# DeltaNet and PReLU feed-forward: the eighth chunk's first product in seven-product form

## The chip, the cores and the metric

The kernel runs on one core of a Trainium2 chip. Its engines are TensorE (PE; PEld is its weight load), VectorE (DVE), ScalarE (ACT), GpSimd (POOL) and SyncE (SP, which issues transfers). The metric is the device time of one execution in microseconds (us), as the median of several runs; lower is better.

## The reference, cut to what matters

```python
batch, n_heads, seq, head_dim = (4, 8, 768, 48)
k_n = k / (np.linalg.norm(k, axis=-1, keepdims=True) + 1e-06)
for t in range(S):
    kt, vt, bt = (k_n[:, :, t], v[:, :, t], beta[:, :, t, None])
    y[:, :, t] = np.einsum('bhd,bhde->bhe', q[:, :, t], state)
    v_old = np.einsum('bhde,bhd->bhe', state, kt)
    state = state + bt[:, :, :, None] * np.einsum('bhd,bhe->bhde', kt, vt - v_old)
# x: y as 3072 tokens of 384; w_in 384 x 2048, w_out 2048 x 384, all float32
h = x @ w_in
g = np.maximum(h, 0.0) + alpha * np.minimum(h, 0.0)
return (g @ w_out).astype(np.float32)
```

A recurrent attention whose state is corrected at each token, then a feed-forward block with a slope `alpha` of its own for each hidden feature below zero.

## The kernel before, in words

The sequence is cut into 12 chunks of 64 positions; with four batches a chunk has 256 tokens. Attention goes through 24 steps `n`, two per chunk (one per pair of batches). Inside a step the recurrence is a triangular system. Four steps share one elimination on DVE (`eliminate`, L594 a product and L600 a sum, 30 times each, then transposes to `turned` and `inverse`, L567), done ahead in small pieces. Each step has a burst A (through the state, outputs, next state: PE L868, L906, L925) and a burst B (L792, L850, and L893, whose result DVE turns into `u` at L897). L792 multiplies with `diag`, which ACT copies from `turned` (L765).

The feed-forward part of chunk c has a first product (`x @ w_in`, 16 blocks of 128 features, taken in eight pairs) and a second (`g @ w_out`). It fills PE between the bursts. `feed_forward` is a generator over all chunks; `stretch` and `weave` lay its pieces, the elimination's pieces and small copies between the bursts at shares written out by hand (`FILL`, `FILLS`: pieces of feed-forward; `PIECES_OF`, `TURNS`: pieces of elimination for the three stretches of a step). All five engines run in the order in which the code issues, so an instruction that waits holds up what is queued behind it on its engine.

The plain first product (`ffn_in`, L1071) has six matmuls of 256 columns per pair; ACT then writes relu(-h) from PSUM (L1081) and DVE forms alpha' times that plus h in two halves (L1083), where alpha' is 1 - alpha. The seven-product form (`ffn_in_fast`) treats two of the three blocks of 128 along the inner dimension as a two by two block product with seven products in place of eight: per pair two matmuls of 256 columns (L1311), three of 128 (L1316) and four shared ones of 128 (L1321) into another PSUM bank `q`. ACT copies these four to SBUF as `z` (L1340), POOL adds them up in three instructions (L1345), DVE adds them to the pair's own PSUM bank to get h (L1350, `total`), ACT writes relu(-h) to `r` (L1355, `below`) and DVE applies the slopes (L1359, `slope`). The list `Due` lays these at steps after the pair. The form needs sums of blocks of `w_in` (`input_sums`, L1238, eight DVE instructions, which write into attention buffers no longer used and into `w_in`) and four sums of tokens (`token_sums`, L1273). One bank `q` serves all pairs but the first, so a pair's shared products wait for ACT's copy of the pair before.

`FAST_IN = 8`: chunks 0 to 7 (the first eight) use the plain form, chunks 8 to 11 the seven-product form. The second products of chunks 2 and later are in a seven-product form of their own (`ffn_out_fast`, L1135, DVE additions L1159, sums of activations L1025; `ffn_out_faster`, L1405 and L1401, behind `ffn_in_fast`). The input sums are made in the second product of chunk 7, every third step.

In `ffn_in_fast` the buffers for `z` alternate between a spare key tile and half of the elimination's `block`, those for `r` between another key tile and `block`'s other half. `rows_y` copies a step's outputs to `xt` in 16 small ACT instructions (L962), behind DVE's transpose `z` (L949).

Of the kernel before, what the change touches and what calls it, by code (L numbers as in the profile page):

```python
# [25 lines left out]
FP32 = mybir.dt.float32  # L26
U32 = mybir.dt.uint32
S8 = mybir.dt.int8
ALU = mybir.AluOpType
# [4 lines left out]
HB = 32  # L34
W_IN_P = 512
BUSY = 8
EARLY = 8
FIRST = 6
NARROW = 8
LATE = 16  # L40
FAST_IN = 8


@with_exitstack
def kernel(
# [11 lines left out]
    nc = tc.nc  # L57

    B, H, S, D = q.shape
# [6 lines left out]
    G = H // 2  # L66
# [4 lines left out]
    const = ctx.enter_context(tc.tile_pool(name="const", bufs=1))  # L71
    work = ctx.enter_context(tc.tile_pool(name="work", bufs=2))
    psum = ctx.enter_context(tc.tile_pool(name="psum", bufs=1, space=bass.MemoryType.PSUM))

    doubles, big, ffn_banks = ExitStack(), [], []
# [54 lines left out]
    k_early = [k_pair[:, 0], k_pair[:, 1], k_last]  # L130
# [169 lines left out]
    for t in range(2):  # L300
# [5 lines left out]
        out=ones, in_=ones, compare_op=ALU.is_ge, fill=1.0, base=0,  # L306
# [7 lines left out]
    for t in range(2):  # L314
# [5 lines left out]
        out=first_of, in_=ident.rearrange("p (q u e) -> p u q e", u=2, e=HB // 2)[:, 0],  # L320
# [39 lines left out]
    inv = [const.tile([128, H, C], FP32, name=f"inv{i}") for i in range(NE)]  # L360
    mid = [const.tile([128, H, C], FP32, name=f"mid{i}") for i in range(2)]

    right = [const.tile([128, H + 1, HB], FP32, name=f"right{i}") for i in range(EARLY)]

    def zeros():

# [162 lines left out]
    NJ = 4  # L529
# [456 lines left out]
    FP = FT // 2  # L986
# [215 lines left out]

    held = {}

    def spare():

        if not held:
            held["same"] = work.tile([128, NJ, H, HB], FP32, name="same", bufs=1)
            for i in range(3):
                held[i] = work.tile([128, G, 128], FP32, name="k_t", bufs=EARLY + 1)  # L1210
        return held

    def input_sum(x, h):

        def four(t):
            return t.rearrange("p h d -> p (h d)").rearrange("p (i e) -> p i e", e=128)

        if x == 0:
            flat = spare()["same"].rearrange("p j h c -> p (j h c)")
            return flat.rearrange("p (i e) -> p i e", e=128)[:, 4 * h : 4 * h + 4]  # L1220
        if x == 1:
            return four(k_early[h])
        return four(k_early[2]) if h == 0 else spare()[0]

    def input_sums():

        for h in range(2):
            own = [
                w_in[:, t].rearrange("p (i f e) -> p i f e", f=2, e=128)[:, 4 * h : 4 * h + 4]
                for t in range(2)  # L1230
            ]
            a11, a12, a21, a22 = own[0][:, :, 0], own[1][:, :, 0], own[0][:, :, 1], own[1][:, :, 1]
            s1, s2, s3 = (input_sum(x, h) for x in range(3))
            for dst, x, y, op in (
                (s1, a21, a22, ALU.add), (s2, s1, a11, ALU.subtract),
                (s3, a11, a21, ALU.subtract), (a21, a12, s2, ALU.subtract),
            ):
                nc.vector.tensor_tensor(out=dst, in0=x, in1=y, op=op)  # L1238
                yield

    class Due:

# [18 lines left out]

    def token_sums(c):

        xt, t = xts[c], spare()[2]

        def x(k, u):
            return xt[:, k, u * 128 : (u + 1) * 128]

        for dst, a, b in (
            (0, x(0, 1), x(0, 0)), (1, x(1, 1), t[:, 0]), (2, x(1, 1), x(0, 1)),  # L1270
            (3, x(1, 0), t[:, 1]),
        ):
            nc.vector.tensor_tensor(out=t[:, dst], in0=a, in1=b, op=ALU.subtract)  # L1273

    def ffn_in_fast(c):
        xt = xts[c]
        gss[c] = [act_of(c, i) for i in range(FP)]
        due = due_of[c] = Due()
        t = spare()[2]

        def x(k, u):
            return xt[:, k, u * 128 : (u + 1) * 128]

        def quarter(flat):
            return flat.rearrange("p (i e) -> p i e", e=128)

        def terms(i):

            if i % 2 == 0:
                return spare()[1]  # L1290
            if "block" not in held:
                held["block"] = work.tile([128, HB * (HB + 1)], FP32, name="block", bufs=1)
            return quarter(held["block"][:, 0:512])

        def pair(i):
            p = ffn_banks[i % 3]
            q = quarter(ffn_banks[2 if i == 0 else 3])
            z, g = terms(i), act_of(c, i)
            if "less" not in held:
                held["less"] = work.tile([128, G, 128], FP32, name="k_t", bufs=EARLY + 1)  # L1300
            r = held["less"] if i % 2 == 0 else quarter(held["block"][:, 512:1024])
            r = r.rearrange("p (f u) e -> p f (u e)", f=2)

            def w(k, f):
                return w_in[:, k, (2 * i + f) * 128 : (2 * i + f + 1) * 128]

            def s(x):
                return input_sum(x, i // 4)[:, i % 4]

            def whole(f):  # L1310
                nc.tensor.matmul(  # L1311
                    p[:, f * 256 : f * 256 + 256], w(2, f), xt[:, 2], start=True, stop=False
                )

            def more(j, a, b):
                nc.tensor.matmul(  # L1316
                    p[:, j * 128 : j * 128 + 128], a, b, start=False, stop=(j > 0)
                )

            def shared(j, a, b):  # L1320
                nc.tensor.matmul(q[:, j], a, b, start=True, stop=True)  # L1321

            def own():
                whole(0)
                yield
                more(0, w(1, 0), x(1, 0))
                more(1, w(0, 1), x(1, 1))
                yield
                whole(1)
                yield  # L1330
                more(2, w(1, 1), t[:, 3])
                yield

            def common():
                shared(0, w(0, 0), x(0, 0))
                shared(1, s(1), t[:, 1])
                yield
                shared(2, s(2), t[:, 2])
                shared(3, s(0), t[:, 0])
                nc.scalar.copy(z, q)  # L1340
                for dst, a, b in (
                    (z[:, 1], z[:, 0], z[:, 1]), (z[:, 2], z[:, 1], z[:, 2]),
                    (z[:, 1::2], z[:, 1:3], z[:, 3:4].to_broadcast([128, 2, 128])),
                ):
                    nc.gpsimd.tensor_tensor(out=dst, in0=a, in1=b, op=ALU.add)  # L1345
                yield

            def total():
                h = g.rearrange("p f i -> p (f i)")
                nc.vector.tensor_tensor(  # L1350
                    out=h, in0=p, in1=z.rearrange("p i e -> p (i e)"), op=ALU.add
                )

            def below():
                nc.scalar.activation(r, g, ACT.Relu, scale=-1.0)  # L1355

            def slope():
                for f in range(2):
                    nc.vector.scalar_tensor_tensor(  # L1359
                        out=g[:, f], in0=r[:, f], scalar=al_t[:, 2 * i + f : 2 * i + f + 1],  # L1360
                        in1=g[:, f], op0=ALU.mult, op1=ALU.add,
                    )

            due.put(PER * (i + 1) + {0: PER, FP - 1: 2}.get(i, 3), total)
            due.put(PER * (i + 2) + {FP - 2: 1, FP - 1: -4}.get(i, 2), below)
            due.put(PER * (i + 2) + {FP - 2: 1, FP - 1: -2}.get(i, 5), slope)
            for gen in (own(), common()) if i == 0 else (common(), own()):
                for _ in gen:
                    due.step()
                    yield  # L1370

        early = operand_sums(0)
        due.put(PER * 6 + 5, lambda: next(early, None))
        rest = chain(early, operand_sums(1))
        for at in (6, 6, 7, 7, 8, 9, 10):
            due.put(PER * FP + at, lambda: next(rest, None))
        for i in range(FP):
            yield from pair(i)
# [604 lines left out]
    )  # L1983

    def feed_forward():
        for c in range(2, FAST_IN):
            yield from ffn_in(c)
            if c < FAST_IN - 1:
                yield from ffn_out_fast(c)
        made = input_sums()  # L1990
        for i, _ in enumerate(ffn_out_fast(FAST_IN - 1)):
            if i > 2 and i % 3 == 0:
                next(made, None)
            if i == FAST_PARTS - 2:
                assert FAST_IN in whole
                token_sums(FAST_IN)
            yield
        for _ in made:
            assert False
        for c in range(FAST_IN, NCH):  # L2000
            yield from ffn_in_fast(c)
            yield from ffn_out_faster(c)
# [10 lines left out]
    for n in range(NJ, JOINED):  # L2013
# [9 lines left out]
        JOINED: (3, WHOLE - 2 * PIECES - 6 - 2 * share - 3, 2 * PIECES),  # L2023
        JOINED + 1: (0, 4, 7), JOINED + 2: (4, 5, 7), JOINED + 3: (1, 1, 6),
    }
    TURNS = [(3, 3, 4), (3, 3, 4), (4, 4, 4), (0, 5, 6)]
    FILL = {JOINED: (8, 12, 12), JOINED + 1: (10, 12, 10), JOINED + 2: (8, 10, 12)}
    FILLS = [(12, 10, 12), (12, 18, 12)]
# [94 lines left out]
```

## Time and profile before

| | |
|---|---|
| median of 3 runs | 631.03 us (630.53 to 634.83) |
| the profiled execution | 630.72 us, of which the span is 629.0 |
| eighth chunk (c = 7), first product | 407.03 to 433.61 us |
| its second product | 433.61 to 453.8 us |
| ninth chunk (c = 8), first product, seven-product form | 453.8 to 479.04 us |
| bursts of steps 16 B, 17 A, 17 B | 407.89, 415.03, 429.93 us |
| bursts of steps 18 A, 18 B, 19 A | 438.81, 454.64, 461.46 us |
| POOL additions L1345 | 96, 56.4 us in all, 28.4 and 28.0 by buffer |

The profile shows, per engine, the busy time; a chain of waits from the end backwards; and a timeline of instructions, with the idle time in front of them and what ended it. A matmul of float32 leaves two records.

### The profile page before, as it was taken

The page shows a single profiled execution, that of the slowest core. Times are in us where ns is not written, and L with a number is a line of the kernel's source. Part 1 is how long each engine was busy: PE and PEld are TensorE (multiplying, and loading weights), DVE is VectorE, ACT ScalarE, POOL GpSimd, SP SyncE. Part 2 cuts the span into 40 slices and gives each one's busy share as a digit, 9 for nine tenths or more (in the row PEclk, how much of TensorE's full clock was granted, in tenths as well). Part 3 has the DMA queues.
Part 4 walks back from the last instruction along what each step waited for, and adds up shares of the span by engine and source line. Part 5 has one row for each costly group of instructions (what it writes and reads, how often), then busy time and mean ns, then how long its engine had stood idle before and what let it go on. Part 6 is the DMA issues. An engine that isn't in the chain of part 4 may idle for free.

```text
span 629.0 us, 21661 instructions
## 1 busy us (share of the span) xinstructions
PE 617.6 (98%) x9116; PEld 546.5 (87%) x9116; DVE 502.5 (80%) x1219; ACT 312.2 (50%) x834; POOL 98.5 (16%) x214
## 2 busy tenths in 40 slices
PE   6999999999999999999999999999999999999997
PEld 5678888566789989989989989989999999999997
DVE  4988898979989988868978868778979578486383
ACT  6878566255545146347346446335356366352230
POOL 7031211010001000000000000000053062071350
PEclk9999999999999999999999999999999999999999
DMA  7968735112243341241332221311220300100100
GB/s 117 302 151 175 253 76 162 29 40 52 41 78 52 63 67 28 55 73 28 54 69 34 43 37 26 56 26 24 49 49 12 62 15 12 29 3 1 26 1 25
DMA packets 145968, 39.26 MB, mean 62 GB/s; under 512 B 139040, under 2 KB 142256, under 8 KB 145872
## 3 DMA queue, kind: packets, MB, share of 16 engines
q1 hardware_dynamic: 144000, 37.40, 29.1%
q8 instruction: 71, 1.16, 0.7%
q10 hardware_dynamic: 1872, 0.49, 0.4%
q14 instruction: 25, 0.20, 0.1%
HBM read 33.14 MB, written 4.72 MB: 60 GB/s over the span
## 4 chain that ended last, share of the span: by engine, by line
PE 89%; DVE 5%; ACT 2%; DMA 1%; SPq 1%; issue 1%; ACTq 0%; DVEq 0%
PE p_ffn L1071 18%; PE p_ffn L1135 10%; PE p_more L1071 8%; PE p_more L1405 8%; PE p_more L1135 8%; PE p_more L1321 5%; PE p_ffn L1114 5%; PE p_ffn L1311 3%; PE p_ffn L1405 3%; PE p_pair L868 3%; PE p_ffn L1316 3%; PE p_pair L906 2%; PE p_pair L792 2%; PE p_pair L502 2%; PE p_pair L850 2%; PE p_pair L728 2%
## 5 line engine op out<-in xcount | busy, mean ns | idle before, releaser
L1071 PE MATMUL p_ffn<-xt,w_in 128*128 128x256 f32 x528 | 123.1, 384 | 0.1
L1071 PEld LDWEIGHTS p_ffn<-xt,w_in 128*128 128x128 f32 x528 | 97.7, 190 | 14.0 <-ACT inv L762 0.4
L962 ACT COPY xt<-z 32x96 f32<-32x96 f32 x240 | 64.5, 269 | 49.6 <-DVE z L949 46.4
L1071 PE MATMUL p_more<-xt,w_in 128*128 128x256 f32 x240 | 55.7, 382 | 0.0
L1345 POOL TENSOR_TENSOR k_t<-k_t 128x128 f32<-128x128 f32 (+1 forms) x48 | 28.4, 592 | 165.8 <-ACT k_t L1340 163.3
L600 DVE TENSOR_TENSOR block<-block,prod 128x30 f32<-128x30 f32 (+9 forms) x150 | 50.0, 333 | 5.1
L1071 PEld LDWEIGHTS p_more<-xt,w_in 128*128 128x128 f32 x240 | 44.9, 190 | 6.3
L594 DVE TENSOR_TENSOR prod<-block 128x30 f32<-128x30 f32 (+9 forms) x150 | 48.6, 324 | 1.3
L419 POOL TENSOR_TENSOR beta_t<-beta_t,rec 128x8 f32<-128x8 f32 x24 | 7.0, 294 | 244.2 <-DVE rec L413 240.1
L1083 DVE SCALAR_TENSOR_TENSOR act<-act,al_t,p_ffn 128x256 f32<-128x256 f32 x72 | 31.0, 471 | 16.3 <-ACT act L1081 16.3
L809 ACT COPY inv<-p_pair 32x256 f32<-32x256 f32 x30 | 10.9, 362 | 59.1 <-DVE u L897 35.5
L1081 ACT ACTIVATE act<-p_ffn 128x512 f32<-128x512 f32 x36 | 21.4, 594 | 25.4 <-PE p_ffn L1071 25.1
L1345 POOL TENSOR_TENSOR block<-block 128x128 f32<-128x128 f32 (+1 forms) x48 | 28.0, 583 | 12.8 <-ACT block L1340 10.3
L1311 PE MATMUL p_ffn<-xt,w_in 128*128 128x256 f32 x96 | 29.3, 387 | 0.0
L1135 PE MATMUL p_ffn<-w_out,act 128*128 128x192 f32 x160 | 27.7, 327 | 0.0
L1135 PEld LDWEIGHTS p_ffn<-w_out,act 128*128 128x128 f32 x160 | 26.2, 190 | 0.3
L897 DVE TENSOR_TENSOR u<-p_pair,wgt 128x384 f32<-128x384 f32 x24 | 13.2, 553 | 16.5 <-PE p_pair L893 9.2
L1083 DVE SCALAR_TENSOR_TENSOR act<-act,al_t,p_more 128x256 f32<-128x256 f32 x40 | 17.3, 474 | 10.9 <-ACT act L1081 10.8
L878 DVE TENSOR_TENSOR r<-v_raw,p_pair 64x192 f32<-64x192 f32 (+1 forms) x66 | 23.2, 352 | 2.1 <-PE p_pair L868 1.0
L1135 PE MATMUL p_more<-w_out,act 128*128 128x192 f32 x128 | 22.3, 326 | 0.0
L1340 ACT COPY k_t<-p_more 128x512 f32<-128x512 f32 x16 | 9.4, 586 | 25.5 <-PE p_more L1321 18.9
L1405 PE MATMUL p_more<-w_out,act 128*128 128x192 f32 x128 | 21.5, 327 | 0.0
(279 smaller groups left out, 1480.8 us busy)
## 6 DMA issues: line engine op xcount, KB each, us to landing
w_out<-in_moe_w_in_dram SPq DMA_DIRECT2D x10, 512.0 KB, 5.6
v_raw<-in_v_dram SPq DMA_DIRECT2D x48, 96.0 KB, 2.8
kl<-in_k_dram SPq DMA_DIRECT2D x96, 48.0 KB, 2.4
out_dram<-o_sb SPq DMA_DIRECT2D x90, 48.0 KB, 1.6
space_out<-in_moe_w_out_dram SPq DMA_DIRECT2D x11, 384.0 KB, 4.5
ke_last<-in_k_dram SPq DMA_DIRECT2D x25, 96.0 KB, 3.3
qp<-in_q_dram SPq DMA_DIRECT2D x64, 32.0 KB, 2.2
w_out<-in_moe_w_out_dram SPq DMA_DIRECT2D x5, 384.0 KB, 6.2
```

The costliest lines, as they stand in the source:

```text
L594: nc.vector.tensor_tensor(out=prod, in0=r[:, 0:j, j : j + 1].to_broadcast([128, j, n]), in1=r[:, j : j + 1, j + 1 : HB].to_broadcast([128, ...
L600: nc.vector.tensor_tensor(out=r[:, 0:j, j + 1 : HB], in0=r[:, 0:j, j + 1 : HB], in1=prod, op=ALU.add)
L878: nc.vector.tensor_tensor(out=r[to, a], in0=v_in[to, a], in1=p[own, a, :, 0:D], op=ALU.subtract)
L962: nc.scalar.copy(to[quad(r), u, bp, t], z[quad(2 * t + u), r])
L1071: nc.tensor.matmul(p_h[:, i], w_in[:, t, (f + i) * 128 : (f + i + 1) * 128], xt[:, t], start=(t == 0), stop=(t == KT - 1),)
L1083: nc.vector.scalar_tensor_tensor(out=g[:, i], in0=g[:, i], scalar=al_t[:, f + i : f + i + 1], in1=p_h[:, i], op0=ALU.mult, op1=ALU.add,)
L1114: nc.tensor.matmul(p_o[u], gs[f // 2][:, f % 2, u * 128 : (u + 1) * 128], w_out[:, f], start=(f == 0), stop=(f == FT - 1),)
L1135: nc.tensor.matmul(p, x(i), w(i), start=(i == 0), stop=(i == FP - 1))
L1311: nc.tensor.matmul(p[:, f * 256 : f * 256 + 256], w(2, f), xt[:, 2], start=True, stop=False)
L1321: nc.tensor.matmul(q[:, j], a, b, start=True, stop=True)
L1345: nc.gpsimd.tensor_tensor(out=dst, in0=a, in1=b, op=ALU.add)
L1405: nc.tensor.matmul(p, x(i), w(i), start=(i == 0), stop=(i == FP - 1))
```

## The change

1. `FAST_IN` goes from 8 to 7: the eighth chunk's first product takes the seven-product form, so the input sums must be made a chunk earlier, in the second product of chunk 6. The two sums that overwrite `w_in` come last, and the eight are laid at steps 1, 3, 5, 8, 11, 14, 18 and 22 in place of every third. The spare tiles are taken one by one when first needed.
2. `z` and `r` of pair i share one buffer, the activation tile of pair i + 2; the last two pairs use the space of two `right` tiles and a key tile. `right` becomes one tile cut into eight.
3. In chunk 7 alone, for the first six pairs, ACT multiplies `r` by the slopes (two instructions), and DVE's `slope` is one addition over both halves.
4. `ffn_banks` is rotated by one before the first chunk of the new form.
5. The elimination's pieces are laid differently in steps 15, 16 and 18: (0, 5, 1), (1, 3, 4), (8, 7, 4) in place of (0, 5, 6), (3, 3, 4), (4, 4, 4).

```diff
-FAST_IN = 8
+FAST_IN = 7
...
-    right = [const.tile([128, H + 1, HB], FP32, name=f"right{i}") for i in range(EARLY)]
+    rights = const.tile([128, EARLY, H + 1, HB], FP32, name="right")
+    right = [rights[:, i] for i in range(EARLY)]
...
     def input_sums():
 
+        last = []
         for h in range(2):
...
                 (s1, a21, a22, ALU.add), (s2, s1, a11, ALU.subtract),
-                (s3, a11, a21, ALU.subtract), (a21, a12, s2, ALU.subtract),
+                (s3, a11, a21, ALU.subtract),
             ):
                 nc.vector.tensor_tensor(out=dst, in0=x, in1=y, op=op)
                 yield
+            last.append((a21, a12, s2))
+        for dst, x, y in last:
+            nc.vector.tensor_tensor(out=dst, in0=x, in1=y, op=ALU.subtract)
+            yield
...
         def terms(i):
 
-            if i % 2 == 0:
-                return spare()[1]
-            if "block" not in held:
-                held["block"] = work.tile([128, HB * (HB + 1)], FP32, name="block", bufs=1)
-            return quarter(held["block"][:, 0:512])
+            if i < FP - 2:
+                return quarter(act[:, i + 2].rearrange("p f i -> p (f i)"))
+            if i == FP - 1:
+                return spare(1)
+            return quarter(rights[:, 0:2].rearrange("p n h i -> p (n h i)")[:, 0:512])
...
-            if "less" not in held:
-                held["less"] = work.tile([128, G, 128], FP32, name="k_t", bufs=EARLY + 1)
-            r = held["less"] if i % 2 == 0 else quarter(held["block"][:, 512:1024])
-            r = r.rearrange("p (f u) e -> p f (u e)", f=2)
+            r = z.rearrange("p (f u) e -> p f (u e)", f=2)
+            scaled = c < FAST_IN + 1 and i < FP - 2
...
             def below():
                 nc.scalar.activation(r, g, ACT.Relu, scale=-1.0)
+                if scaled:
+                    for f in range(2):
+                        nc.scalar.mul(r[:, f], r[:, f], al_t[:, 2 * i + f : 2 * i + f + 1])
 
             def slope():
+                if scaled:
+                    nc.vector.tensor_tensor(out=g, in0=r, in1=g, op=ALU.add)
+                    return
                 for f in range(2):
...
     def feed_forward():
+        made, m = input_sums(), FAST_IN - 1
+        at = {(m, 1): (1, 3, 5, 8, 11, 14, 18, 22)}
         for c in range(2, FAST_IN):
...
+            for k, passes in enumerate((ffn_in(c), ffn_out_fast(c))):
+                for i, _ in enumerate(passes):
+                    if i in at.get((c, k), ()):
+                        next(made)
+                    if (c, k, i) == (m, 1, FAST_PARTS - 2):
+                        assert FAST_IN in whole
+                        token_sums(FAST_IN)
+                    yield
         for _ in made:
             assert False
+        ffn_banks.append(ffn_banks.pop(0))
         for c in range(FAST_IN, NCH):
             yield from ffn_in_fast(c)
             yield from ffn_out_faster(c)
...
+    PIECES_OF.update({15: (0, 5, 1), 16: (1, 3, 4), 18: (8, 7, 4)})
```

More of the change, by code (lines that the diff above doesn't have):

```diff
@@ L1203, with spare @@
     held = {}
[L1205 to L1211, printed above, removed]
+    def spare(i):
+        if i not in held:
+            held[i] = (
+                work.tile([128, NJ, H, HB], FP32, name="same", bufs=1) if i == "same"
+                else work.tile([128, G, 128], FP32, name="k_t", bufs=EARLY + 1)
+            )
+        return held[i]
     def input_sum(x, h):
@@ L1218, in input_sum @@
         if x == 0:
-            flat = spare()["same"].rearrange("p j h c -> p (j h c)")
+            flat = spare("same").rearrange("p j h c -> p (j h c)")
             return flat.rearrange("p (i e) -> p i e", e=128)[:, 4 * h : 4 * h + 4]
@@ L1222, in input_sum @@
             return four(k_early[h])
-        return four(k_early[2]) if h == 0 else spare()[0]
+        return four(k_early[2]) if h == 0 else spare(0)
     def input_sums():
+        last = []
         for h in range(2):
@@ L1262, in token_sums @@
     def token_sums(c):
-        xt, t = xts[c], spare()[2]
+        xt, t = xts[c], spare(2)
         def x(k, u):
@@ L1278, in ffn_in_fast @@
         due = due_of[c] = Due()
-        t = spare()[2]
+        t = spare(2)
         def x(k, u):
@@ L1985, in feed_forward @@
     def feed_forward():
+        made, m = input_sums(), FAST_IN - 1
+        at = {(m, 1): (1, 3, 5, 8, 11, 14, 18, 22)}
         for c in range(2, FAST_IN):
[L1987 to L1997, printed above, removed]
+            for k, passes in enumerate((ffn_in(c), ffn_out_fast(c))):
[6 more added lines that the diff above has]
+                    yield
         for _ in made:
             assert False
+        ffn_banks.append(ffn_banks.pop(0))
         for c in range(FAST_IN, NCH):
```

## The prediction

> **What bounds the kernel now.** The page's first part comes first, then the chain that ended last, in order of time. Columns of the chain: start, length, what (one matmul leaves two records).
>
> ```profile
> PE 617.6 (98%) x9116; PEld 546.5 (87%) x9116; DVE 502.5 (80%) x1219; ACT 312.2 (50%) x834; POOL 98.5 (16%) x214
> ...
> 421.30 5.18 PE p_ffn L1071 x24
> ...
> 454.64 0.68 PE p_pair L792 x50
> ...
> 465.84 0.43 PE p_ffn L1311 x2
> ...
> 468.27 0.43 PE p_ffn L1311 x2
> ```
>
> From 100 us on PE hardly idles. A plain first product costs 5.18/24 = 0.216 us a record. One seven-product pair runs from 465.84 to 468.27, 2.43 us. So PE's work is the bound, and only as long as DVE, ACT and POOL deliver in time. Busy time by stage tells how close they are. The first two rows are the eighth chunk's first product, the third is its second product, the fourth the ninth chunk's first product, already in the new form. Columns: PE, PEld, DVE, ACT, POOL.
>
> ```profile
> 407.00:427.00 20.00, 20.00 (x301) 17.26 (x300) 15.35 (x38) 6.87 (x18) 0.00 (x0) 1.00 0.19 39
> 427.00:434.00 7.00, 7.00 (x154) 6.08 (x153) 6.02 (x16) 3.48 (x10) 0.00 (x0) 1.00 0.20 25
> 434.00:454.00 20.00, 20.00 (x208) 19.60 (x207) 19.26 (x45) 9.34 (x33) 0.00 (x0) 1.00 0.19 31
> 454.00:479.00 25.00, 25.00 (x496) 23.50 (x496) 19.75 (x39) 15.29 (x37) 13.70 (x24) 1.00 0.23 42
> ```
>
> DVE is full in the third row, and POOL is idle in the first three. The timeline of DVE, ACT and POOL gives the deadlines and what POOL does to DVE. Columns: start, length, engine, line, operation, and in brackets the idle time before it and what ended it.
>
> ```profile
> 449.75 0.59 DVE L567 STREAM_TRANSPOSE turned<-block 128x256 f32<-128x256 f32 x1
> ...
> 467.47 1.35 DVE L1359 SCALAR_TENSOR_TENSOR act<-block,al_t,act 128x256 f32<-128x256 f32 x2
> ...
> 472.01 1.58 DVE L1359 SCALAR_TENSOR_TENSOR act<-block,al_t,act 128x256 f32<-128x256 f32 x2
> ...
> 478.45 0.87 DVE L1359 SCALAR_TENSOR_TENSOR act<-block,al_t,act 128x256 f32<-128x256 f32 x2
> ```
>
> ```profile
> 450.37 0.41 ACT L765 COPY diag<-turned 128x256 f32<-128x256 f32 x1 [1.34 <-DVE turned L567]
> ```
>
> ```profile
> 466.54 2.00 POOL L1345 TENSOR_TENSOR block<-block 128x128 f32<-128x128 f32 x3 [2.37 <-ACT block L1340]
> ...
> 471.46 1.85 POOL L1345 TENSOR_TENSOR block<-block 128x128 f32<-128x128 f32 x3 [0.65 <-ACT block L1340]
> ```
>
> The last elimination's result reaches `diag` at 450.78, and step 18's burst on PE (L792) wants it at 454.64: 3.86 us to spare. A pair of slopes (L1359, both tensors in SBUF) takes 0.87 us with POOL at rest and 1.35 and 1.58 beside POOL's additions at 466.54 and 471.46.
>
> **The change part by part.**
>
> PE. The eighth chunk's first product has 96 records, 96 x 0.2157 = 20.70 us without the attention bursts. In the new form it is what the twelfth chunk shows, which has no burst in it: from 587.89, where the second product before it ends, to 607.30, 19.41 us. Gain 1.3 us, all of it on the path. The number of weave steps is 48 in both forms, so the bursts fall at the same places.
>
> ACT. Added: eight copies of shared products (L1340, 0.586) and twelve scalings by alpha; for these the nearest row is L762, 128x256 with a per-partition scale, 0.51. That is 4.7 + 6.1 = 10.8 us where ACT is busy 10.35 of 27 us: covered as a sum. The order is less comfortable. ACT's queue has three copies of `xt` ahead of the sixth pair's copy of shared products, they wait for DVE's transpose `z`, and pair 7's shared products on PE wait for that one bank. In the ninth chunk the same copy ends at 471.39 and PE wants the bank at 472.23: 0.84 us to spare.
>
> POOL. 24 additions, 8 x 1.8 = 14.4 us, in a stage where POOL was idle. Their own cost is hidden by that; what they cost DVE is priced below.
>
> Input sums. Eight of 0.60 us (start to start, L1238) move to the seventh chunk's second product. By the instruction order, five elimination steps fewer lie in that stretch. From the solve of step 15 to that of step 16 DVE's work goes from 18.5 to 18.9 us (rows times spacings) in 24.7 us: hidden by its idle time, 0.4 us if that cover were gone. The buffers they write have no later reader in the attention part; the queue of transfers keeps its order. Nothing.
>
> Buffers. Shared products go to later activation tiles, `right` becomes one tile with the same addresses, the banks are rotated by one so that the numbering fits one chunk less. A pair's buffer is no longer reused two pairs later, which takes waits away and adds none on PE; the addition that overwrites a tile comes after the slope that reads it on the same engine. Nothing; at worst one POOL addition late, 0.46 us.
>
> DVE, from the solve of step 16 (409.65) to the fourth transpose `turned`. Added: seven elimination steps (deferred from the stretches before) at 0.75 = 5.2; eight totals at 0.60, six one-piece slopes at 0.60 and two old pairs at 0.79 in place of eight pairs at 0.79, +3.7; three output additions that now precede it, 0.27 each, +0.8. Removed: five input sums, -3.0. Net +6.7 us. To swallow it there are the 3.86 us above, less the 1.3 by which PE comes sooner, and DVE's idle 1.96 + 0.67 + 1.15 + 0.15 = 3.9 us; but the first total must wait for the first shared products and POOL's additions. In the ninth chunk it starts 4.3 us after the solve, DVE has 3.2 us of work until then, so 1.0 us stays idle. 6.7 - 2.5 - 2.9 = 1.3 us short. The wait is PE's, at step 18's burst, and behind it stands the ninth chunk.
>
> DVE beside POOL. In that stretch 25 DVE instructions with two SBUF operands (18 of the elimination, 6 slopes, one sum) fall where POOL adds. The ninth chunk's eight pairs of slopes take 0.87, 1.35, 1.08, 1.58, 1.54, 0.87, 0.88, 0.88: 2.1 us over 8 x 0.87, or 0.13 an instruction; 25 x 0.13 = 3.3. Elimination steps beside POOL's copies early in the kernel are nearer in kind but not in what POOL does: L600 took 0.440 in place of 0.349 and 0.450 in place of 0.378 us, 0.08 more; with the 40 in 64 slopes that met POOL, 25 x 0.63 x 0.08 = 1.3. Upper end: the 40 slopes beside POOL average 0.710 us against 0.478 for the other 24, 25 x 0.232 = 5.8. Lower end 0: DVE may wait anyway. I take the middle of the two nearer rows, 2.3 us, since most of the 25 are elimination instructions and the POOL work is that of the slopes' row.
>
> The Trainium skill, page "SBUF — State Buffer", section "SBUF: two separate sides", says that VectorE instructions with two SBUF inputs and GpSimd instructions exclude each other on one pair of ports, for a whole instruction. The trace agrees: the totals (L1350), with one operand in PSUM, keep 0.68 us beside POOL. By that rule every one of the 25 would pay like the slopes that met POOL, and the sum would end near the upper end.
>
> Sum, against the profiled execution (630.72 us, span 629.0 and 1.7 around it; 0.3 below the median 631.03): -1.3 + 1.3 + 2.3 = +2.3, **633.0 us**.
>
> **The rivals.**
>
> Cover holds (not slower). DVE's idle time and spare take all of it, say because the lock costs nothing beyond waits that exist and the deferred steps fit. For it: before, DVE ran 2.2 us behind PE (output additions at 450.78 for products that ended at 448.57) and PE did not wait. Against it: the 1.3 us are short before any contention. 630.72 - 1.3 = 629.4 us, up to 630.4.
>
> POOL and DVE exclude each other fully. 25 x 0.232: 630.72 - 1.3 + 1.3 + 5.8 = 636.5 us. For it: the slopes' rows. Against: elimination instructions are shorter, and some of their waiting falls into waits between a product and the sum that needs it.
>
> ACT's order binds. DVE's `z` comes 1.2 us later than in the ninth chunk, relative to PE, which is 0.4 over the 0.84 to spare, and 14 of the 25 instructions precede it (1.3 us): PE waits 1.7 us at pair 7's shared products, and afterwards DVE catches up. 630.72 - 1.3 + 1.7 = 631.1 us.
>
> The change not doing what it says is no rival with weight: PE's instruction order has the 24 further matmuls, and the form's time is measured in four chunks.
>
> **How the numbers follow.** Forecast 0.45, its own range 631.5 to 635.5 (lock 0.8 to 4.8); cover holds 0.30; ACT's order 0.10; full exclusion 0.15. The range 629.2 to 636.0 leaves out about half of the full exclusion and 0.1 of tails. One per cent, 6.3 us, is about what a measurement of this kernel can tell from no change: faster than 624.7 would need a gain that PE's records do not hold, 0.01; slower than 637.3 only beyond the full exclusion, 0.05; within, 0.94.
>
> **What would show it.** Right: L1071 down by 96 records and the seven-product lines up by 144; PE's chain broken at L792 in step 18 by `diag` and DVE's `turned`, perhaps earlier at pair 7's shared products; elimination rows (prod, block) between 412 and 433 us longer than now; DVE without idle time from there to 455. Wrong: no idle PE between 407 and 460, or waits of PE anywhere before 400, which nothing here foresees. What would overturn the sum is the DVE count: a few instructions that overlap more than their spacings say.

## The result, and the profile after

The changed kernel takes 635.28 us (median of 8 runs, 633.87 to 637.31) against 631.12 us before (8 runs, 630.09 to 634.83): ratio 1.0061, interval 1.0037 to 1.0085. The profiled execution took 633.87 us, of which the span is 632.2. So it got slower by about 4 us; 633.0 was forecast.

The shares of the chain that ended last, in the page of the kernel before, and then the page of the changed kernel: first part, shares of the chain and the plain product's row:

```profile
PE 89%; DVE 5%; ACT 2%; DMA 1%; SPq 1%; issue 1%; ACTq 0%; DVEq 0%
```

```profile
PE 617.5 (98%) x9164; PEld 547.6 (87%) x9164; DVE 510.6 (81%) x1225; ACT 322.0 (51%) x854; POOL 113.6 (18%) x238
...
PE 84%; DVE 7%; ACT 4%; POOL 1%; issue 1%; SPq 1%; DMA 1%; DVEq 0%; POOLq 0%; ACTq 0%
...
L1072 PE MATMUL p_ffn<-xt,w_in 128*128 128x256 f32 x480 | 112.2, 384 | 0.0
```

PE has 48 records more and the same busy time, so the product did become cheaper. But the chain that ended last now goes through DVE for 7% of the span, before for 5%. That is a hint and no measure: in the fastest version below it is 10%. Line numbers have moved: most lines are one further down (L893 is L894, L949 is L950, L1159 is L1160, L1071 is L1072), L1401 and L1405 are L1412 and L1416, and the seven-product lines L1311, L1316, L1321, L1340, L1345, L1350, L1355 and L1359 are L1316, L1321, L1326, L1345, L1350, L1355, L1360 and L1370; L1363 is ACT's scaling, L1367 the slope in one piece.

The same stretches as before, the last one cut short, in the windows view (columns: length, busy time and instructions of PE, PEld, DVE, ACT, POOL, then clock, DMA share, GB/s):

```profile
407.00:427.00 20.00, 18.17 (x332) 16.94 (x331) 17.21 (x37) 12.12 (x28) 9.49 (x16) 1.00 0.22 40
427.00:434.00 7.00, 7.00 (x166) 6.55 (x165) 6.48 (x12) 6.75 (x17) 5.03 (x9) 1.00 0.12 16
434.00:454.00 20.00, 18.83 (x199) 18.02 (x199) 18.99 (x48) 10.35 (x35) 0.55 (x1) 1.00 0.10 19
454.00:460.00 6.00, 5.02 (x146) 4.41 (x145) 5.90 (x18) 1.13 (x3) 0.00 (x0) 1.00 0.45 76
```

PE, full in all of them before, now idles 1.83 + 1.17 + 0.98 = 4.0 us. The waits between 380 and 470 us name the places (columns: who waits, for whom, us in total, times, longest):

```profile
PE p_ffn L1326 <- ACT act L1345: 1.8, 1, 1.8
PE p_ffn L1416 <- DVE act L1370: 1.2, 1, 1.2
PE p_pair L793 <- ACT diag L766: 1.0, 1, 1.0
ACT diag L766 <- DVE turned L568: 5.8, 1, 5.8
```

Three waits: pair 7's shared products for ACT's copy of the pair before, the second product for the last slopes, step 18's burst for `diag`. The chain of waits, and then a row of ACT's timeline, show who is behind the first and the last of them:

```profile
424.56 0.58 DVE z L950
...
426.02 0.59 ACT act L1345
...
456.74 0.53 DVE turned L568
457.30 0.41 ACT diag L766
457.75 0.72 PE p_pair L793 x48
```

```profile
425.17 0.83 ACT L963 COPY xt<-z 32x96 f32<-32x96 f32 x3 [2.07 <-DVE z L950]
```

ACT's copy at 426.02 stands in its queue behind three copies of `xt`, which wait for DVE's `z`. Ahead of the last `turned`, DVE has no idle time over 0.1 us from 436.14 on. So the first and the third wait are DVE's. Ahead of the second the chain goes through ACT as well: after the late copies of `xt`, ACT is busy for 6.75 of the 7.00 us in the second window above, more than DVE.

**A finer measure.** The time moves by several us between executions (630.09 to 634.83 before), in the traces mostly in the first 80 us. From one step's solve on PE (L894) to the next, executions of one form agree to a few hundredths of a us from step 9 on. Three intervals are touched; all others from step 9 on are equal before and after.

| us | 15 to 16 | 16 to 17 | 17 to 18 | sum |
|---|---|---|---|---|
| before | 24.70 | 22.04 | 24.71 | 71.45 |
| after | 24.71 | 23.10 | 27.44 | 75.25 |

That is +3.80. The ninth chunk, in the same form and without waits, has 20.91 and 24.52 for the steps that lie alike, 1.32 us less than 22.04 + 24.71 before. So the form saves 1.32 us of PE, and waits cost 5.1.

### The profile page after: what moved, and what is told of

Read it like the earlier page. It is cut to its first block, busy times and chain, and to the rows that moved or that the text cites. A ratio compares the mean times of both kernels' runs of the same rounds, so it can differ in the third digit from the quotient of the medians.

```text
span 632.2 us, 21808 instructions
## 1 busy us (share of the span) xinstructions
PE 617.5 (98%) x9164; PEld 547.6 (87%) x9164; DVE 510.6 (81%) x1225; ACT 322.0 (51%) x854; POOL 113.6 (18%) x238
## 4 chain that ended last, share of the span: by engine, by line
PE 84%; DVE 7%; ACT 4%; POOL 1%; issue 1%; SPq 1%; DMA 1%; DVEq 0%; POOLq 0%; ACTq 0%
PE p_ffn L1072 16%; PE p_ffn L1136 8%; PE p_more L1072 7%; PE p_ffn L1416 7%; PE p_more L1136 7%; PE p_more L1416 5%; PE p_ffn L1115 5%; PE p_ffn L1326 4%; PE p_more L1316 3%; PE p_pair L869 2%; PE p_more L1321 2%; PE p_pair L503 2%; PE p_pair L907 2%; PE p_pair L793 2%; PE p_ffn L1316 2%; PE p_pair L729 2%
## 5 line engine op out<-in xcount | busy, mean ns | idle before, releaser
L1072 PE MATMUL p_ffn<-xt,w_in 128*128 128x256 f32 x480 | 112.2, 384 | 0.0
L1072 PEld LDWEIGHTS p_ffn<-xt,w_in 128*128 128x128 f32 x480 | 88.7, 190 | 12.8 <-ACT inv L763 0.4
L1350 POOL TENSOR_TENSOR act<-act 128x128 f32<-128x128 f32 (+1 forms) x90 | 51.6, 578 | 161.7 <-ACT act L1345 157.0
L595 DVE TENSOR_TENSOR prod<-block 128x30 f32<-128x30 f32 (+9 forms) x150 | 49.7, 332 | 1.4
L1072 PE MATMUL p_more<-xt,w_in 128*128 128x256 f32 x192 | 44.5, 382 | 0.0
L1072 PEld LDWEIGHTS p_more<-xt,w_in 128*128 128x128 f32 x192 | 35.9, 190 | 5.0
L1370 DVE SCALAR_TENSOR_TENSOR act<-act,al_t 128x256 f32<-128x256 f32 x48 | 30.7, 678 | 0.1
L1316 PE MATMUL p_more<-xt,w_in 128*128 128x256 f32 x100 | 30.7, 389 | 0.0
L1416 PE MATMUL p_ffn<-w_out,act 128*128 128x192 f32 x160 | 29.2, 330 | 1.2 <-DVE act L1370 1.2
L1416 PEld LDWEIGHTS p_ffn<-w_out,act 128*128 128x128 f32 x160 | 25.9, 190 | 2.1 <-DVE act L1370 1.5
L1345 ACT COPY act<-p_ffn 128x512 f32<-128x512 f32 x25 | 14.6, 585 | 24.1 <-PE p_ffn L1326 23.9
L1136 PE MATMUL p_ffn<-w_out,act 128*128 128x192 f32 x128 | 22.4, 327 | 0.0
L1084 DVE SCALAR_TENSOR_TENSOR act<-act,al_t,p_more 128x256 f32<-128x256 f32 x32 | 13.8, 474 | 9.7 <-ACT act L1082 9.6
L1115 PE MATMUL p_ffn<-w_out,act 128*128 128x384 f32 x64 | 21.5, 489 | 0.0
```

Of the source, the lines that this page charges most:

```text
L595: nc.vector.tensor_tensor(out=prod, in0=r[:, 0:j, j : j + 1].to_broadcast([128, j, n]), in1=r[:, j : j + 1, j + 1 : HB].to_broadcast([128, ...
L1072: nc.tensor.matmul(p_h[:, i], w_in[:, t, (f + i) * 128 : (f + i + 1) * 128], xt[:, t], start=(t == 0), stop=(t == KT - 1),)
L1084: nc.vector.scalar_tensor_tensor(out=g[:, i], in0=g[:, i], scalar=al_t[:, f + i : f + i + 1], in1=p_h[:, i], op0=ALU.mult, op1=ALU.add,)
L1115: nc.tensor.matmul(p_o[u], gs[f // 2][:, f % 2, u * 128 : (u + 1) * 128], w_out[:, f], start=(f == 0), stop=(f == FT - 1),)
L1136: nc.tensor.matmul(p, x(i), w(i), start=(i == 0), stop=(i == FP - 1))
L1316: nc.tensor.matmul(p[:, f * 256 : f * 256 + 256], w(2, f), xt[:, 2], start=True, stop=False)
```

## The experiments

Theory: DVE has too much to do between the solve of step 16 and step 18's burst, and POOL makes its instructions longer. Rivals: POOL's share is most of it; ScalarE's order is the bound; the other edits cost something by themselves. The sums below are of the three intervals, each from one profiled execution. Each ratio is to the kernel before, timed again beside the run (medians 631.5 to 632.14 us), so ratios compare better than times.

**The old pieces.** The line with the new `PIECES_OF` is taken out.

```diff
-    PIECES_OF.update({15: (0, 5, 1), 16: (1, 3, 4), 18: (8, 7, 4)})
```

> The changed kernel with the elimination's pieces back where they were (steps 15, 16 and 18 as before), so seven elimination steps, 5.2 us of DVE, leave the stretch from step 16's solve to the last transpose of the elimination. Theory (DVE's serial work up to that transpose binds): the wait of step 18's burst for diag, 1.0 us or more in the changed kernel's trace, is gone, the wait of pair 7's shared products may stay in part (0.5 to 1.8 us), and the time comes to 630 to 632.5 us. Rival (ScalarE's order or POOL's additions bind by themselves): the time stays at 634 us or more.

638.19 us, ratio 1.0092 (1.0076 to 1.0109); sum 76.04. The theory's expectation failed, and the time is the rival's (634 us or more). The wait for `diag` is gone (17 to 18 takes 24.52), but 16 to 17 takes 26.38, and 15 to 16, where the input sums now stand beside the old pieces, 25.14 against 24.70. The waits of this kernel, and its windows behind the first:

```profile
PE p_ffn L1326 <- ACT act L1345: 3.5, 1, 3.5
```

```profile
432.00:434.00 2.00, 0.00 (x0) 0.00 (x0) 2.00 (x5) 1.19 (x4) 0.00 (x0) 1.00 0.69 112
434.00:436.00 2.00, 1.75 (x9) 1.75 (x10) 1.37 (x4) 1.93 (x6) 1.56 (x3) 0.67 0.47 54
436.00:438.00 2.00, 2.00 (x8) 1.73 (x8) 1.97 (x5) 1.94 (x5) 1.21 (x4) 0.50 0.18 22
438.00:440.00 2.00, 2.00 (x76) 1.85 (x74) 1.97 (x5) 1.60 (x5) 0.60 (x1) 0.97 0.00 0
```

The deferred pieces did not cause the loss; they had shifted part of it from pair 7 to `diag`. Here PE's granted clock also fell, to 0.50, for some 3.4 us after the idle time: 26.38 - 20.91 = 5.47 us lost for a wait of 3.50.

**No additions by POOL in the eighth chunk.** POOL's 24 additions there are left out, so its output lacks them.

```diff
-                for dst, a, b in (
+                for dst, a, b in () if c == FAST_IN else (
```

> The changed kernel without POOL's 24 additions in the eighth chunk; the shared products are added unsummed there, so that chunk's output is another. Theory (POOL and DVE exclude each other): the elimination's rows in that chunk take their length from before (0.40 us for 128x240 where they now take up to 0.84), PE's waits fall from about 5 us to about 1.3, and the time comes to 630 to 632 us. Rival (DVE has too many instructions, the meeting with POOL costs little): 634 to 636 us.

634.75 us, ratio 1.0036 (1.0023 to 1.0049); sum 74.28, 1.0 under the changed kernel. That is the rival's time. DVE's groups of the slope in one piece (all six) and of the elimination in 411 to 432 us (columns: busy time, mean ns, idle time ahead), first with POOL (the changed kernel), then without:

```profile
L1367 DVE TENSOR_TENSOR act<-act 128x512 f32<-128x512 f32 x6 | 5.1, 852 | 0.5 <-ACT act L1363 0.5
...
L595 DVE TENSOR_TENSOR prod<-block 128x228 f32<-128x228 f32 (+3 forms) x8 | 4.3, 544 | 0.0
L601 DVE TENSOR_TENSOR block<-block,prod 128x228 f32<-128x228 f32 (+4 forms) x9 | 4.0, 447 | 0.3
```

```profile
L1367 DVE TENSOR_TENSOR act<-act 128x512 f32<-128x512 f32 x6 | 4.1, 685 | 1.0 <-ACT act L1363 0.9
...
L601 DVE TENSOR_TENSOR block<-block,prod 128x228 f32<-128x228 f32 (+5 forms) x10 | 4.0, 399 | 0.3
L595 DVE TENSOR_TENSOR prod<-block 128x228 f32<-128x228 f32 (+5 forms) x10 | 3.9, 389 | 0.1
```

By these means POOL's cost to DVE is 6 x 0.167 + 8 x 0.155 + 9 x 0.048 = 2.7 us (the shapes in a group differ a little). Matched one by one between the two timelines it is 2.6 us: of 22 instructions ten are longer, by 0.13 to 0.46 us, and the others take the same time to 0.01. Only 1.0 us reaches PE, and in that is also the 0.62 us for which DVE stood for POOL's additions ahead of the first total. With POOL at rest pair 7 still waits 0.8, the second product 1.2 and `diag` 1.0 us.

**`rows_y` later.** In step 17 all 16 pieces go into the third stretch.

```diff
...
+                if n == 17:
+                    extra[2].append((part(rows, 16), 16, 0.3))
...
```

> The changed kernel with all sixteen copies of xt of step 16's outputs in step 17's last stretch, so that none stands ahead of the sixth pair's copy of shared products on ScalarE. Theory (DVE's serial work binds at step 18's burst): pair 7's shared products no longer wait (1.8 us less), and the later waits grow by as much; the time stays within 1 us of the changed kernel, 634 to 636. Rival (the waits add up, ScalarE's order is a cost of its own): 1.8 us less, 633 to 633.8 us.

635.54 us, ratio 1.005 (1.0032 to 1.0067); sum 74.45, 0.8 under the changed kernel; the time is the theory's. Pair 7's wait is gone, and 16 to 17 falls to 21.89. 17 to 18 rises to 27.85: the second product now waits 0.8 and 0.5 us for slopes and `diag` is 1.0 us late as before. ScalarE's order had handed DVE's lateness to PE early, and without it most of the lateness comes out further on.

**The slopes by DVE.** `scaled = False`: DVE does two instructions a pair, ScalarE none.

> The changed kernel with the eighth chunk's slopes on DVE in two halves as in the later chunks, so ScalarE loses twelve scalings (5.5 us) and DVE gains six instructions and 1.1 us. Theory (DVE binds): 1 to 2.5 us slower than the changed kernel, 636 to 638 us. Rival (ScalarE's order binds): faster than the changed kernel, 633 to 634 us.

636.13 us, ratio 1.0055 (1.0041 to 1.0068); sum 76.64, 1.4 over the changed kernel, with 2.6 us of wait at pair 7. The ratios of the two (1.0055 and 1.0061) can't be told apart; the intervals can. Work that is given to ScalarE there is a gain; DVE binds.

**Pieces and rows together.** Old pieces with late rows; half of the pieces put off with late rows; half of them with the rows of the change.

```diff
-    PIECES_OF.update({15: (0, 5, 1), 16: (1, 3, 4), 18: (8, 7, 4)})
+    PIECES_OF.update({15: (0, 5, 4), 16: (2, 3, 4), 18: (5, 6, 4)})
```

> The changed kernel with the old pieces of the elimination (15: 0, 5, 6; 16: 3, 3, 4; 18: 4, 4, 4) and, in step 17, all 16 pieces of rows_y in the third stretch. Steps are measured from one solve on PE to the next; before: 15-16 24.70, 16-17 22.04, 17-18 24.71, sum 71.45; the changed kernel 75.26; old pieces alone 76.04. If DVE's queue at two places is what costs (pair 7's copies behind z, and diag behind turned), then both are relieved together here: no wait for diag, pair 7's wait from 3.5 us to under 1.5 us, PE's granted clock not falling behind it, sum 71.5 to 73, time 631.3 to 632.8, within 1 us of the kernel before. If the work of the seven-product form on DVE is too much for steps 16 and 17 in whatever order, the wait moves again and the sum stays at 74 or more, time 634 or more.

> As the run before, but with half of the elimination put off (15: 0, 5, 4; 16: 2, 3, 4; 18: 5, 6, 4: three pieces later instead of seven). If DVE's queue at the two places is what costs: pair 7's wait under 1 us, wait for diag under 0.5 us, sum of the three steps 71 to 73, time 631 to 632.8. If the work is too much in whatever order: 74 or more, 634 or more.

> Three pieces put off instead of seven (15: 0, 5, 4; 16: 2, 3, 4; 18: 5, 6, 4), rows_y where the changed kernel has it. If the pieces only shift DVE's work between the two places: pair 7's wait between 1.8 and 3.5 us (2.5), the wait for diag under 0.5 us, sum 73.5 to 75.5, time 633.5 to 635.5. If the granted clock falls behind the longer wait of pair 7, as with the old pieces, the sum is at the upper end or above.

The first: 634.03 us, ratio 1.0032 (1.0016 to 1.0048), sum 73.58. The second: 633.46, 1.0019 (1.0006 to 1.0032), sum 73.13. The third: 636.13, 1.005 (1.0031 to 1.007), sum 74.27. The first two miss the ranges of the sum by 0.6 and 0.1 us and those of the time by 1.2 and 0.7. The third has the sum and the waits that were expected (2.5 us at pair 7, none for `diag`), and its time is 0.6 over the range. In the first two `diag` no longer waits, and what is left sits with the pairs' totals and slopes. Of the 3.8 us about half went.

**The other edits alone.** `FAST_IN = 8` and the old pieces; later tiles, order of the input sums, turn of the banks and ScalarE's slopes stay, which now fall on the ninth chunk. Then the same with `scaled = False`.

> Everything of the change but the eighth chunk's seven-product form and the pieces: shared products of the later chunks' pairs in activation tiles, slopes of the chunk after by ScalarE, sums of the input weights in the new order, a turn of the banks. If only the seven-product form of the eighth chunk with its DVE and POOL work costs, every step is within 0.3 us of the kernel before, sum 71.2 to 71.8, time 630.5 to 631.7. If the later tiles or ScalarE's slopes cost by themselves, steps from 19 on (the first chunk in the form here) get longer by 1 us or more.

> The other edits without the eighth chunk's seven-product form and without the slopes by ScalarE: later tiles, order of the sums of the input weights, turn of the banks. With the slopes by ScalarE step 19-20 was 25.64 against 24.52 before, with a wait of 0.9 us for a slope of DVE. If ScalarE's scaling (two instructions more in a row ahead of its other work) is what delays that slope: 24.52 here, time 630.5 to 632, no change from before. If the later tiles or the turn of the banks cost it: 25.3 or more here too.

633.05 us, ratio 1.0014 (1.0 to 1.0028): the three intervals are those of before, but 19 to 20 takes 25.64 against 24.52, as the second alternative had it. With slopes by DVE: 631.53 us, 1.0001 (0.9989 to 1.0013), every interval from step 9 on as before. So later tiles, the order of the sums and the banks cost nothing, and ScalarE's slopes cost 1.1 us in the ninth chunk, where DVE has room, and save 1.4 in the eighth, where it has none.

**Pieces forward.** The elimination goes into step 15's first two stretches, where DVE idles; with late rows, then with the rows of the change.

```diff
-    PIECES_OF.update({15: (0, 5, 1), 16: (1, 3, 4), 18: (8, 7, 4)})
+    PIECES_OF.update({15: (4, 6, 3), 16: (1, 2, 3), 18: (5, 5, 4)})
```

> The changed kernel with pieces of the elimination moved forward instead of back (15: 4, 6, 3; 16: 1, 2, 3; 18: 5, 5, 4), into step 15's first two stretches, where DVE has 2.7 us of idle between 380 and 390 us, and step 17's 16 pieces of rows_y in its third stretch. If DVE's own work between steps 16 and 18 is what costs, and not its place beside POOL or ScalarE's order: 15-16 24.7, 16-17 21.0 to 21.8, 17-18 24.5 to 25.3, sum 70.2 to 71.8 (before 71.45, with half the pieces put off 73.13), time 630.5 to 632.5, at least 1.3 us under the run with half the pieces put off. If the waits come from DVE beside POOL or from ScalarE's order, the sum stays at 72.5 or more and the time at 633 or more.

> The same pieces moved forward, rows_y where the changed kernel has it. If DVE's work before z of step 17 is what pair 7's wait comes from, 2 to 3 us less of it ahead of z takes most of that wait (1.8 us in the changed kernel) with rows_y in place too: 16-17 21.0 to 22.0, 17-18 24.5 to 25.5, sum 70.5 to 72, time 630.8 to 632.5. If rows_y ahead of z is needed for the wait whatever the pieces do: 16-17 stays at 23 or more, sum 73 or more.

634.2 us, ratio 1.0033 (1.0021 to 1.0046), sum 72.95; and 634.36 us, 1.0045 (1.0031 to 1.0059), sum 74.52 with a wait of 2.4 us at pair 7. What was expected of DVE's work failed in both, and the figures are those of the other alternatives. The waits of the one with late rows show why:

```profile
DVE act L1355 <- POOL act L1350: 4.9, 2, 3.2
...
DVE u L898 <- PE p_pair L894: 2.9, 2, 1.8
...
PE p_ffn L1316 <- DVE act L1355: 0.8, 1, 0.8
```

DVE came early to `u` of step 16 and stood 1.8 us for PE's solve, then 1.7 us for the first total (414.58 to 416.27; the 3.2 us in the row are at 461, in step 18). The work moved forward had only made DVE wait longer: in the changed kernel it stood 1.64 and 0.62 us at these two places. Between the first total and `z` of step 17 there were still four elimination steps, as many as in the changed kernel (from 414.64, 418.68, 420.93 and 423.81).

**Into the idle time.** One elimination step in place of four between the first total and `z`; of the other three, by the timelines, two go ahead of `u` of step 16 and one behind `u` of step 17. The edit is against the run with pieces forward and late rows, and the rows stay late.

```diff
-    PIECES_OF.update({15: (4, 6, 3), 16: (1, 2, 3), 18: (5, 5, 4)})
+    PIECES_OF.update({15: (4, 6, 5), 16: (3, 0, 2), 17: (1, 3, 4), 18: (5, 6, 4)})
```

> As the run with pieces moved forward and rows_y late, with the pieces put where DVE was seen idle there (1.84 us ahead of u of step 16, 1.68 us ahead of the first pair's total, 1.2 us at the end of step 18's elimination): 15: 4, 6, 5; 16: 3, 0, 2; 17: 1, 3, 4; 18: 5, 6, 4. Between the first pair's total and z of step 17 one elimination step is left of four. If what pair 7 waits for is DVE's work between u of step 16 and z of step 17, and work ahead of u only made DVE idle longer: 16-17 falls from 22.47 to 20.9 to 21.6, 17-18 is 25.0 to 25.8, sum 70.7 to 72.1, time 630.8 to 632.8, no slower than before within 0.2%. If the waits come from DVE's work beside POOL in the pairs themselves (totals and slopes), which no order of pieces changes: sum 72.5 or more, time 633 or more.

631.04 us, ratio 0.9989 (0.9972 to 1.0005); intervals 25.42, 20.91, 24.52, sum 70.85, 0.6 under before. PE's only wait listed between 380 and 470 us, and the windows over the former three places:

```profile
PE p_ffn L1316 <- DVE o_sb L1160: 0.5, 1, 0.5
```

```profile
420.00:430.00 10.00, 10.00 (x77) 9.59 (x77) 9.70 (x19) 8.27 (x18) 6.06 (x11) 1.00 0.35 52
430.00:440.00 10.00, 10.00 (x235) 9.45 (x237) 9.86 (x22) 8.31 (x24) 3.25 (x4) 1.00 0.01 3
440.00:450.00 10.00, 10.00 (x111) 9.86 (x100) 9.66 (x26) 6.67 (x25) 0.00 (x0) 1.00 0.14 23
```

16 to 17 and 17 to 18 are those of the ninth chunk without waits, to the hundredth, with POOL adding beside DVE as in the changed kernel. The alternative, that the pairs' totals and slopes beside POOL make the waits in any order, is refuted. DVE's idle time ahead of the first total was not filled (1.69 us, 1.68 before the edit). What changed is that `z` of step 17 comes 12.94 us after `u` of step 16, in place of 15.48 in the changed kernel. What remains is 0.7 us at step 16: PE waits for the output additions (L1160), and two elimination steps more than in the run with pieces forward stand ahead of them. This version is about 4 us faster than the change and cannot be told from before: its interval holds 1.

## Why the prediction was right, and where it was not

**PE.** Predicted -1.3 us, found 1.32. The plain product lost 96 records (L1071 768, L1072 672) and the seven-product lines gained 144 (576 to 720), as said.

**DVE's serial work.** The step that was mis-sized: "6.7 - 2.5 - 2.9 = 1.3 us short". The waits sum to 5.1 us; without POOL's additions they are still 74.28 - 71.45 + 1.32 = 4.15. The sum pooled all spare time from the solve of step 16 to the last `turned` against one deadline. There are nearer ones: `z` of step 17, for pair 7, and the last slopes, for the second product. Spare time at the end cannot serve them, nor could idle time ahead of the first total, where the order had no work. So the prediction had the place wrong too: it put the wait at step 18's burst, with pair 7 as a "perhaps earlier", and only 0.98 of PE's 4.0 us of idle time stand at that burst. The last run shows this: the same instructions in another order, with three elimination steps fewer between the first total and `z`, leave none of the three waits. It has the late rows as well; against the run with pieces forward, which has them too, the order of the pieces alone is worth 72.95 - 70.85 = 2.1 us. The cost of the input sums is as forecast: nothing in the changed kernel, and 0.44 us in 15 to 16 with the old pieces, where "0.4 us if that cover were gone" was said.

**DVE beside POOL.** Predicted +2.3 us. As DVE time it was 2.6, or 0.12 for each of 22 instructions, against the 0.13 read from the nearer row. On the path it was 1.0, and in the last run, where DVE is not late, nothing. The step that failed is the one from DVE's time to PE's. The rows show the elimination stretched beside POOL, in the timelines of DVE and POOL of the changed kernel (start, length):

```profile
411.57 0.65 DVE L595 TENSOR_TENSOR prod<-block 128x228 f32<-128x228 f32 x1
...
430.68 0.84 DVE L595 TENSOR_TENSOR prod<-block 128x228 f32<-128x228 f32 x1
```

```profile
411.46 5.62 POOL L1350 TENSOR_TENSOR act<-act 128x128 f32<-128x128 f32 x9 [38.35 <-ACT act L1345]
...
429.21 2.06 POOL L1350 TENSOR_TENSOR right<-right 128x128 f32<-128x128 f32 x3 [0.50 <-ACT right L1345]
```

Without POOL such products take 0.39 us on average (L595 above). The rule of the Trainium skill, page "SBUF — State Buffer", section "SBUF: two separate sides", that one of the two waits for a whole instruction of the other, fits these two rows: the second is 0.46 us longer than without POOL, about one of POOL's additions (L1345 before, 0.46). The eight totals (L1355), with one operand in PSUM, are the same with POOL and without, to 0.01 us. That every instruction pays so is not borne out: ten of the 22 pay, and the mean is 0.12 against 0.232.

The two errors had opposite signs, 1.3 for 4.1 and 2.3 for 1.0, so the forecast of 633.0 came out 2.3 us low in the median and 0.9 in the profiled execution, within the range. That it lies so near is partly luck: neither term had its size.

**The rivals.** Cover holds is refuted for this order: PE waits 4 us in plain sight. In the order of the last run it does hold from step 16 to step 18. Full exclusion is refuted as a price (1.0 us on the path), though its time, 636.5, was not far. ACT's order: its place was real, and its price too, 1.7 forecast and 1.83 measured. What failed is "afterwards DVE catches up". With the rows late that wait goes and most of the loss stays (a sum of 74.45 against 75.25), so the order is where DVE's lateness first shows, not its cause.

**What would show it.** `diag` and `turned` at L793 broke the chain, pair 7's shared products earlier; the elimination's rows got longer. DVE without idle from 412 to 455 was not quite so: it stood 0.62 us for the first total, 0.45 at 427.66 and 0.32 at 435.81.

**Left open.** PE's idle time is 4.0 us and the intervals lose 5.1. The difference comes with each wait: 23.10 - 20.91 - 1.83 = 0.36 us for the one at pair 7, 27.44 - 24.52 - 2.15 = 0.77 for the two in 17 to 18, 0.36 and 0.27 for the two of the run with half of the pieces put off. It is put down to matmul ends, which are modelled, at the edges of each wait; this was not tested. Nor was a version tried that takes the last 0.7 us at step 16.

## What to carry to other kernels

Spare time can be pooled only up to the next instruction that another engine waits for: list every such deadline in the queue and do the sum for each. In this kernel, moving filler work earlier helped only where it left the stretch in which the engine was late; moved within what lay ahead of that stretch, it just lengthened an idle time already there. Taking away the wait that a profile shows first may only uncover the next one of the same backlog, so compare intervals between fixed points of the program, not waits.

## What the runs showed of the hardware that was not expected

A single wait of PE can cost more than its length. After 3.50 us idle (old pieces) the granted clock fell to 0.5 for some 3.4 us, and 5.47 us were lost. With the pieces moved forward and the rows of the change the same came after 2.42 us (427.63 to 430.05): 16 to 17 took 25.25, 4.34 over 20.91. Windows of that kernel:

```profile
430.00:432.00 2.00, 1.95 (x10) 1.86 (x11) 1.47 (x3) 1.93 (x6) 1.77 (x3) 0.64 0.42 50
432.00:434.00 2.00, 2.00 (x8) 1.78 (x7) 1.97 (x5) 1.94 (x5) 1.26 (x4) 0.51 0.01 4
434.00:436.00 2.00, 2.00 (x80) 1.82 (x81) 1.97 (x4) 1.57 (x6) 0.48 (x2) 1.00 0.00 0
```

By these rows 2 x 0.36 + 2 x 0.49 = 1.7 us of clock are missing, most of the 1.92 us that were lost beyond the wait; the slow stretch is worked out from this as 1.7/0.5 = 3.4 us. Idle times of 2.45 us (half of the pieces put off) and 2.63 us (slopes by DVE) left the clock at 1.00. The window in which the first of them ended and the next:

```profile
430.00:432.00 2.00, 1.44 (x11) 1.39 (x12) 1.47 (x4) 1.94 (x4) 1.26 (x3) 1.00 0.44 53
432.00:434.00 2.00, 2.00 (x17) 1.93 (x15) 1.96 (x4) 1.93 (x5) 1.37 (x3) 1.00 0.12 14
```

So for idle times of 2.4 to 2.6 us it depends on something else than the length. The Trainium skill, page "TensorE: Matmul & The Clock Gate", section "What's actually happening", speaks of free-running windows of about 3.4 us, of which an idle one throttles the clock. That the position in such a window decides, and that the slow stretch lasts about as long, fits these runs; that 2.42 us were enough does not fit a window that must be idle throughout.
